# Chunk columns by transposing transfers out of SBUF, row factors by VectorE, inverse sums in halves

## The chip, the cores and the metric

The kernel runs on one core of a Trainium2 chip. The metric is the device time of one execution in microseconds, the median of several runs. TensorE is called PE, VectorE DVE, ScalarE ACT, GpSimd POOL and SyncE SP; SP computes nothing here and issues nearly all transfers (DMAs).

## The reference

With x of 2048 rows by 512 columns (bf16), `xn = layernorm(x)` and `out = x + A(xn) * silu(B(xn))`.

A is sliding-window attention with 32 heads of 16 and a window of eight keys at distances 0, 2, ..., 14:

```python
qkv = xn @ wqkv
logits = einsum("bhsd,bhswd->bhsw", q, k[window]) * 16**-0.5      # -1e9 before row 0
o = einsum("bhsw,bhswd->bhsd", softmax(logits), v[window])
A = o @ wo
```

B is an MLP whose hidden columns are shifted along the rows in four groups (by +1, -1, +2 and -2):

```python
h = gelu(layernorm(xn) @ w1)          # 512 x 512
x1 = xn + shifted(h) @ w2             # 512 x 512
B = x1 + gelu(layernorm(x1) @ w3) @ w4   # 512 x 1376, 1376 x 512
```

## The kernel before, in words

Rows are split by parity, so that a distance of 2 becomes 1 within a half: `xn[0]` holds the 1024 even rows, `xn[1]` the odd ones. Each half has two chunks of 512 rows, four tiles of 128. Chunks 0 and 1 are the even rows, 2 and 3 the odd ones.

The first stage works chunk by chunk. `Norm` takes statistics on DVE (`stats`), the reciprocal root on POOL for chunks 1 to 3 (`root`), and scales on DVE (`apply`). The projections need xn with columns on the partitions, `xnT`; `turn` makes it, two tiles at a time, with eight PE transposes into PSUM and one DVE copy. From xnT come q (`q_all`), k (`k_all`, kept by four ACT instructions with head masks, `kM`), and v (`v_pair`, kept in one of two staging tiles `vst` and written to DRAM as `v_d`). Since B normalises xn a second time, each row gets a further factor: `rows2` computes it on POOL, `rows2_spread` transposes the 128 x 4 factors on PE, copies them with DVE, writes them to DRAM (`r2_d`) and reads them back onto all partitions. `rows2_here` instead multiplies the factors into an identity on DVE and spreads them with a matmul of ones. `scaled` multiplies xnT by them, and `w1` uses the result.

`w2(c)` adds the shifted product to xn in place and takes the statistics of the sum. `columns(c)` scales these rows, writes them to DRAM (`x1n_dram`) and reads them back with one transposing transfer as `x1nT`, which `w3` uses. After `w3(3)` comes the attention stage.

The attention stage is a loop over n of 18 units of 114 queries, nine per half. In iteration n run `scores(n)`, ACT's exponentials, DVE's `band`, `values` of an earlier unit, and pieces of w4 and of the output projection (`g_fin`) between them. The sums of the softmax are gathered for batches of four units (the last batch has two). At the end of a batch (n = 5, 9, 13, 16) `inverse` takes the reciprocal, `write_rec` sends it to DRAM, `read_rec` brings it back spread over the partitions into `rr_t`, and `apply` multiplies it into `oT`; the output projection of the rows follows. The last batch of two units goes through PE (`expand`) after the loop, behind `apply(3)`.

The tile framework keeps each engine's instructions in the order in which they are written, and inserts waits between engines where data depends. SP's queue is also in that order, so a transfer that waits holds up all SP transfers behind it. PSUM has eight banks: three pairs go round (`pair`) in the first stages and two single ones (`single`).

Of the kernel before, what the change touches and what calls it, by code (L numbers as in the profile page):

```python
# [8 lines left out]
AF = mybir.ActivationFunctionType  # L9
# [11 lines left out]
def kernel(  # L21
# [19 lines left out]
    def pin(ins):  # L41

        return tc.keep_in_program_order(ins)
# [52 lines left out]
    def single():  # L96
        cnt["s"] += 1
        return PS[:, 6 + (cnt["s"] - 1) % 2, :]
# [54 lines left out]
    m57 = const.tile([P, QB], BF16, name="m57")  # L153
    e_sb = const.tile([P, 8, 8, 16], BF16, name="e_sb")
    zero = const.tile([P, D], BF16, name="zero")

    def head_masks():
        pin(DVE.tensor_reduce(
# [39 lines left out]
    r2_d = dram.tile([NCH, CH], BF16, name="r2_d")  # L198
    x1n_dram = dram.tile([S, D], BF16, name="x1n_dram")
    vst = [b4([P, 2, 2, D], f"vst{i}") for i in range(2)]  # L200


# [4 lines left out]
    def small_t(name, shape, dt=F32):  # L207
        return small.tile(shape, dt, name=name, tag=name)
# [33 lines left out]
    def x_of(c):  # L242
        p, k = c // 2, c % 2
        return xn[p][:, k * TPC : (k + 1) * TPC, :]
# [3 lines left out]
    def rows2(c, ln):  # L248

        r2 = small_t("r2", [P, TPC])  # L250
        r2b = small_t("r2b", [P, TPC], BF16)
        eng = DVE if c == 0 else POOL
        pin(eng.tensor_tensor(out=r2, in0=ln.rstd, in1=ln.rstd, op=ALU.mult))
        pin(eng.tensor_tensor(out=r2, in0=r2, in1=ln.mv[:, :, 1], op=ALU.mult))
        if c == 0:
            pin(ACT.activation(r2, r2, AF.Sqrt, bias=eps_t[:]))
            with nc.allow_low_precision("bf16 row factors"):
                pin(DVE.reciprocal(out=r2b, in_=r2))
        else:
            rsqrt_eps(r2, r2)  # L260
            pin(POOL.tensor_copy(out=r2b, in_=r2))
        r2s[c] = r2b

    def rows2_spread(c):
        pt = single().bitcast(BF16)[0:TPC, 0:P]
        pin(PE.transpose(pt, r2s[c], ident[:]))
        t = small_t("r2t", [TPC, P], BF16)
        pin(DVE.tensor_copy(out=t, in_=pt))
        pin(SP.dma_start(out=r2_d[c].rearrange("(j q) -> j q", q=P), in_=t))
        xn2Ts[c] = b4([P, ND, CH], "xn2T")  # L270
        pin(SP.dma_start(out=xn2Ts[c][:, ND - 1, :], in_=r2_d[c : c + 1, :].to_broadcast([P, CH])))

    def rows2_here(c):

        xn2Ts[c] = t = b4([P, ND, CH], "xn2T")
        d = t[:, 0, :].rearrange("p (j q) -> p j q", q=P)
        pin(DVE.tensor_tensor(
            out=d, in0=ident.unsqueeze(1).to_broadcast([P, TPC, P]), in1=r2s[c].unsqueeze(2).to_broadcast([P, TPC, P]),
            op=ALU.mult,
        ))  # L280
        pt = single()
        pin(PE.matmul(pt, lhsT=ones_bf[:], rhs=t[:, 0, :], start=True, stop=True))
        if c == 0:
            pin(ACT.activation(t[:, ND - 1, :], pt, AF.Copy))
        else:
            pin(DVE.tensor_copy(out=t[:, ND - 1, :], in_=pt))

    def scaled(c):
        p, k = c // 2, c % 2
# [17 lines left out]
    def turn_one(c, t):  # L307
        p, k = c // 2, c % 2
        i = k * TPC + t
        pt = single().bitcast(BF16)[:, 0 : ND * P].rearrange("p (a q) -> p a q", a=ND)  # L310
        for dt in range(ND):
            pin(PE.transpose(pt[:, dt, :], xn[p][:, i, dt * P : (dt + 1) * P], ident[:]))
        pin(ACT.activation(xnT[p][:, :, i * P : (i + 1) * P], pt, AF.Copy))

    def q_half(pts, lo, hi, nts=range(ND)):
        for nt in nts:
# [28 lines left out]
    def k_pad(p):  # L345
        pin(POOL.memset(kM[p][:, :, 0:8, :], 0.0))
        pin(POOL.memset(kM[p][:, :, M + 8 : MK, :], 0.0))
# [35 lines left out]
        else:  # L383
            later.append(put)

    def v_pair(p, t):
        pt = pair()
        for i in range(2):
            v_mm(p, t + i, pt[:, i, :])
        v_keep(p, t, 2, pt[:, 0, :])  # L390

    def v_pad(p):
        rows = v_d[p].rearrange("r e d -> (r e) d")
# [49 lines left out]
    def columns(c):  # L443
        ln = ln2[c]
        ln.apply(0, TPC)
        pin(SP.dma_start(
            out=x1n_dram[c * CH : (c + 1) * CH, :].rearrange("(i q) d -> q i d", q=P), in_=ln.dst
        ))
        x1nT = b4([P, ND, CH], "x1nT")
        pin(SP.dma_start_transpose(out=x1nT, in_=x1n_dram[c * CH : (c + 1) * CH, :]))  # L450
        x1nTs[c] = x1nT

    h3a, h3b = {}, {}
# [39 lines left out]
    pin(POOL.memset(zero, 0.0))  # L493
    k_pad(0)
    k_pad(1)
    pin(ACT.activation(
# [26 lines left out]
    head_masks()  # L523
    load_x(3, 0, 2)
    load_x(3, 2, 2)
    q_half(pq, 2 * P, CH, (0, 1))
    rows2_here(0)
    q_half(pq, 2 * P, CH, (2, 3))
    for a in range(2):
# [4 lines left out]
    l1.stats(2, 4)  # L534
    l1.root()
    l1.apply(0, 4)
    rows2(1, l1)
    pin(SP.dma_start(out=w2_sb, in_=B_w2.rearrange("(g q) n -> q g n", q=P)))
    k_all(0, (0,))
    v_pair(0, 2)  # L540
    k_all(0, (1,))
    v_pad(0)
    w1(0, 0)
    rows2_spread(1)
    pin(SP.dma_start(out=w3_sb, in_=B_w3.rearrange("(dt q) f -> q dt f", q=P)))
    turn(1, 0)
    turn(1, 1)
    w1(0, 1)
    l2 = Norm(x_of(2), x_of(2), TPC, "l1")
    l2.stats(0, 4)  # L550
    l2.root()
    l2.apply(0, 4)
    rows2(2, l2)
    l3 = Norm(x_of(3), x_of(3), TPC, "l1")
    l3.stats(0, 4)
    l3.root()
    scaled(1)
    q_all(1)
    k_all(1)
    v_pair(0, 4)  # L560
    l3.apply(0, 4)
    rows2(3, l3)
    v_pair(0, 6)
    rows2_spread(2)
    w1(1, 0)
    turn(2, 0)
    turn(2, 1)
    w1(1, 1)
    scaled(2)
    q_all(2)  # L570
    turn(3, 0)
    turn(3, 1)
    k_all(2)
    pin(SP.dma_start(
        out=w4_sb[:, 0 : NF - 1, :],
        in_=B_w4[0 : (NF - 1) * P, :].rearrange("(ft q) n -> q ft n", q=P),
    ))
    pin(SP.dma_start(out=w4_sb[0:FL, NF - 1, :], in_=B_w4[(NF - 1) * P : F, :]))
    rows2_here(3)
    scaled(3)  # L580
    w1(2, 0)
    w1(2, 1)
    w1(3, 0)
    w1(3, 1)
    w2(0)
    columns(0)
    v_pad(1)
    q_all(3)
# [96 lines left out]
    def read_rec(b):  # L685
        pin(SP.dma_start(
            out=rr_t.rearrange("p j a q -> p (j a q)"),
            in_=ap_of(rec_ds[b][:], [[16 * NQ, 16], [0, 8], [1, 16 * NQ]]),
        ))

    def apply(b):
        lo, hi = batches[b]
        n = lo
        while n < hi:
            p, u = n // UP, n % UP
            m = min(hi, (p + 1) * UP) - n
            x = oT[p][:, :, u * NQ : (u + m) * NQ].rearrange("p a (j q) -> p a j q", q=NQ)
            rr = rr_t[:, n - lo : n - lo + m].rearrange("p j a q -> p a j q")
            pin(DVE.tensor_tensor(out=x, in0=x, in1=rr, op=ALU.mult))
            n += m  # L700
# [177 lines left out]
    for n in range(NU):  # L878
        now["n"] = n
        q = W4 * (n + 1) // NU - given  # L880
        given += q
        extra = small_g.get(n, [])
        if n == 0:
            w4_take(HEAD)

        if n - 1 in ends:
            read_rec(ends[n - 1])
        if n == 15:
            values(13)
# [7 lines left out]
        if n in xo_at:  # L897
            load_xo(*xo_at[n])
        if n == 4:
            load_wo()  # L900
        if n - 1 not in ends:
            flush_stores(n - 2)
        flush(vstores)
# [88 lines left out]
```

## Time and profile before

| | before |
|---|---|
| median of 3 runs | 197.72 us (197.51 to 197.74) |
| profiled execution | 197.26 us |
| its span, first to last instruction | 195.5 us |
| granted PE clock | 0.996 |
| busy PE, DVE, ACT, POOL | 185.5, 117.8, 133.3, 19.1 us |
| DMA | 28.12 MB in 33576 packets |

The stages of the span: the first projections, w1 and w2 up to 70.8 us, w3 (with the last w2) from 70.8 to 112.4, attention with w4 from there to about 185, and the last output groups to the end. In rows of the profile an instruction is named by its line and engine, then output <- inputs; a count follows with x, and brackets hold the idle time of the engine before it and what ended that.

### The profile page before, as it was taken

The numbers are of one execution on the slowest core, as the hardware profiler recorded it, in microseconds if no ns is written. First come the engines' busy times: TensorE is split into PE (matmuls) and PEld (weight loads), VectorE is DVE, ScalarE is ACT, GpSimd is POOL, SyncE is SP. The second block draws the span as 40 slices with busy tenths as digits, with TensorE's granted clock in tenths as the row PEclk, the third lists the DMA queues.
The fourth block names the chain that finished last, engine by engine and source line by source line (L and its number), as shares of the span: only waits on it lengthen the run. The fifth ranks groups of instructions, "written<-read, shape, count | busy, mean of one in ns | idle before, by whom it ended". The sixth has DMA issues, their size and how long they took to land.

```text
span 195.5 us, 5255 instructions
## 1 busy us (share of the span) xinstructions
PE 185.5 (95%) x2253; PEld 91.8 (47%) x2283; DVE 117.8 (60%) x229; ACT 133.3 (68%) x151; POOL 19.1 (10%) x57
## 2 busy tenths in 40 slices
PE   7899999999999999999999999999999999999990
PEld 2474544554444444444444444445444544554540
DVE  5785767236076697494200035556487888798894
ACT  7399769649817615435656588877887876887871
POOL 3006066100002022006000000000000000000000
PEclk9999999999999999999999999999999999999998
DMA  4997480654000433752480051457565556582523
GB/s 131 339 368 239 132 282 15 218 158 157 0 0 3 136 83 109 215 107 65 110 260 0 0 162 60 157 166 232 153 216 161 137 155 215 127 247 51 171 91 126
DMA packets 33576, 28.12 MB, mean 144 GB/s; under 512 B 10760, under 2 KB 32528, under 8 KB 33552
## 3 DMA queue, kind: packets, MB, share of 16 engines
q1 hardware_dynamic: 33408, 27.71, 47.2%
q8 instruction: 18, 0.29, 0.6%
q10 hardware_dynamic: 144, 0.07, 0.1%
q14 instruction: 6, 0.05, 0.1%
HBM read 17.01 MB, written 8.67 MB: 131 GB/s over the span
## 4 chain that ended last, share of the span: by engine, by line
PE 85%; DMA 5%; DVE 4%; issue 2%; SPq 1%; ACT 1%
PE PS L469 19%; PE PS L328 19%; PE PS L764 19%; PE PS L427 5%; PE PS L811 4%; PE PS L795 4%; PE PS L652 3%; DMA wqk_sb<-in_A_wqkv_dram 3%; PE PS L626 3%; PE PS L362 3%; DMA x1nT<-x1n_dram 2%; PE PS L318 2%; PE PS L662 2%; PE PS L302 2%; DVE sg L825 2%
## 5 line engine op out<-in xcount | busy, mean ns | idle before, releaser
L469 PE MATMUL PS<-x1nT,w_sb 128*128 128x512 bf16 (+1 forms) x173 | 38.2, 379 | 0.4 <-DMA x1nT<-x1n_dram 0.3
L633 ACT ACTIVATE prob<-PS 128x1824 bf16<-128x1824 f32 x18 | 30.4, 1688 | 4.4 <-PE PS L626 3.6
L764 PE MATMUL PS<-w_sb,h3a 128*128 128x512 bf16 x112 | 29.2, 379 | 1.9 <-issue 1.7
L475 ACT ACTIVATE h3a<-PS 128x1024 bf16<-128x1024 f32 x16 | 16.4, 1024 | 21.0 <-PE PS L469 19.1
L777 DVE TENSOR_TENSOR xn<-PS,xn 128x512 bf16<-128x512 f32 x15 | 10.3, 686 | 32.0 <-PE PS L764 31.8
L469 PEld LDWEIGHTS <-w_sb 128*128 128x128 bf16 (+1 forms) x176 | 17.5, 100 | 20.9 <-issue 0.7
L328 PE MATMUL PS<-xnT,wqk_sb 128*128 128x512 bf16 x109 | 25.0, 379 | 0.2
L354 ACT ACTIVATE kM<-PS,em 128x1024 bf16<-128x1024 f32 x16 | 20.8, 1404 | 3.2 <-PE PS L328 3.2
L638 DVE TENSOR_TENSOR prob<-prob,maskb 128x1824 bf16<-128x1824 bf16 x18 | 19.8, 1102 | 1.8 <-ACT prob L633 1.8
L764 PEld LDWEIGHTS <-h3a 128*128 128x128 bf16 x128 | 11.3, 97 | 13.4 <-issue 1.2
L328 PEld LDWEIGHTS <-wqk_sb 128*128 128x128 bf16 x112 | 10.9, 98 | 12.8
L435 DVE TENSOR_TENSOR xn<-PS,xn 128x1024 bf16<-128x1024 f32 x8 | 9.6, 1213 | 11.3 <-PE PS L427 11.3
L811 PE MATMUL PS<-wo_sb,oT 128*128 128x512 bf16 (+1 forms) x68 | 15.5, 366 | 0.0
L328 PE MATMUL PS<-xn2T,w_sb 128*128 128x512 bf16 x62 | 14.6, 379 | 0.1
L427 PE MATMUL PS<-w_sb,hT 128*128 128x512 bf16 x63 | 14.4, 379 | 0.1
L821 ACT ACTIVATE sg<-PS 128x512 bf16<-128x512 f32 (+1 forms) x17 | 9.6, 572 | 6.1 <-PE PS L811 6.1
L764 PE MATMUL PS<-w_sb,h3b 128*128 128x512 bf16 (+1 forms) x44 | 12.8, 380 | 0.8 <-issue 0.8
L339 ACT ACTIVATE qT<-PS 128x1024 bf16<-128x1024 f32 x8 | 8.1, 1024 | 7.6 <-PE PS L328 7.6
L373 ACT ACTIVATE vst<-PS 128x512 bf16<-128x512 f32 (+1 forms) x12 | 8.8, 743 | 3.5 <-ACT sig L784 2.3
L221 DVE BATCH_NORM_STATS2 l1s<-xn 128x6 f32<-128x512 bf16 x16 | 10.1, 680 | 1.6 <-DMA xn<-in_A_x_dram 1.6
L400 ACT ACTIVATE hT<-PS 128x1024 bf16<-128x1024 f32 x8 | 8.1, 1031 | 3.8 <-PE PS L328 3.8
L221 DVE BATCH_NORM_STATS2 l3s<-xn 128x6 f32<-128x512 bf16 x16 | 10.2, 682 | 0.2
(105 smaller groups left out, 229.2 us busy)
## 6 DMA issues: line engine op xcount, KB each, us to landing
ring<-v_d SPq DMA_DIRECT2D x18, 256.0 KB, 3.3
v_d<-vst SPq DMA_DIRECT2D x16, 256.0 KB, 2.7
x1n_dram<-xn SPq DMA_DIRECT2D x4, 512.0 KB
xo<-in_A_x_dram SPq DMA_DIRECT2D x8, 256.0 KB, 4.1
ring<-rec_d SPq DMA_DIRECT2D x4, 456.0 KB, 4.7
out_dram<-xo SPq DMA_DIRECT2D x7, 256.0 KB
xn<-in_A_x_dram SPq DMA_DIRECT2D x6, 256.0 KB, 7.9
w_sb<-in_B_w_dram SPq DMA_DIRECT2D x1, 1376.0 KB
```

The costliest lines, as they stand in the source:

```text
L221: pin(DVE.bn_stats(out=self.st[:, j, :], in_=self.src[:, j, :]))
L328: pin(PE.matmul(pt[:, b, :], lhsT=w[:, dt, nt * P : (nt + 1) * P], rhs=rhs[:, dt, :], start=(dt == 0), stop=(dt == ND - 1),))
L354: pin(ACT.activation(kM[p][:, 2 * a : 2 * a + 2, 8 + k * CH : 8 + (k + 1) * CH, e], pt, AF.Copy, scale=em[:, e : e + 1]))
L427: pin(PE.matmul(pt[:, j, :], lhsT=w2_src(p, g, m0), rhs=w2_sb[:, g, :], start=(g == 0), stop=(g == ND - 1),))
L435: pin(DVE.tensor_tensor(out=xs, in0=pts[h], in1=xs, op=ALU.add))
L469: pin(PE.matmul(pt[:fs, ft % 2, :], lhsT=w3_sb[:, dt, ft * P : ft * P + fs], rhs=x1nT[:, dt, :], start=(dt == 0), stop=(dt == ND - 1),))
L475: pin(ACT.activation(t[:, o : o + 2, :], pt, AF.Gelu_apprx_tanh))
L633: pin(ACT.activation(pr, S_ps[:, :, 0 : ND * NQ], AF.Exp, scale=SCALE))
L638: pin(DVE.tensor_tensor(out=f, in0=f, in1=maskb[:], op=ALU.min))
L764: pin(PE.matmul(pt, lhsT=h3_of(c, ft)[:fs, jj * P : (jj + 1) * P], rhs=w4_sb[:fs, ft, :], start=(ft == 0), stop=(ft == NF - 1 and silu < 2),))
L777: pin(DVE.tensor_tensor(out=x_i, in0=pt, in1=x_i, op=ALU.add))
L811: pin(PE.matmul(pt[:, 0:W], lhsT=oT[p][:, dt, i * P : (i + 1) * P], rhs=wo["sb"][:, dt, c], start=(dt == 0), stop=(dt == ND - 1),))
```

## The change

- xnT of chunks 1 to 3 is made by `turn_dma`: one transposing transfer per tile, SBUF to SBUF, issued by SP. `turn` on PE remains for chunk 0 alone.
- `columns` transposes each tile straight from SBUF, four transfers of 128 x 512 instead of one write to DRAM and one transposing read of 512 x 512. `x1n_dram` is gone.
- Row factors of chunks 1 to 3 are put into a zeroed tile `r2p`, transposed in blocks of 32 by DVE and written to DRAM (`rows2_write`), and read back spread (`rows2_read`). Chunk 3 no longer uses `rows2_here`.
- The order of the first stage is new: v of tiles 4 to 7 comes before q and k of chunk 1; the writes of v are collected in `vputs` and issued after the transposes; w2_sb is loaded earlier and w3_sb later; `w2(0)` stands before `w1(3, 1)`.
- In the attention loop `read_rec` and `apply` work on two units at a time, one iteration apart, for batches 0 to 2. Batch 2's second half is applied at the end of n = 16. The writes of v, the loads of x for the output and the stores stand at the end of the iteration.

```diff
+    r2p = const.tile([P, NCH, 32], BF16, name="r2p")
...
-    def rows2_spread(c):
-        pt = single().bitcast(BF16)[0:TPC, 0:P]
-        pin(PE.transpose(pt, r2s[c], ident[:]))
-        t = small_t("r2t", [TPC, P], BF16)
-        pin(DVE.tensor_copy(out=t, in_=pt))
-        pin(SP.dma_start(out=r2_d[c].rearrange("(j q) -> j q", q=P), in_=t))
+    def rows2_write(c):
+        t = small_t("r2t", [P, 32], BF16)
+        pin(DVE.transpose(out=t, in_=r2s[c]))
+        pin(SP.dma_start(out=ap_of(r2_d[c], [[32, P // 32], [P, 32], [1, 32]]), in_=t))
+
+    def rows2_read(c):
         xn2Ts[c] = b4([P, ND, CH], "xn2T")
...
+    def turn_dma(c, lo=0, hi=TPC):
+        p, k = c // 2, c % 2
+        for t in range(lo, hi):
+            i = k * TPC + t
+            pin(SP.dma_start_transpose(out=xnT[p][:, :, i * P : (i + 1) * P], in_=xn[p][:, i, :]))
...
     def columns(c):
         ln.apply(0, TPC)
-        pin(SP.dma_start(
-            out=x1n_dram[c * CH : (c + 1) * CH, :].rearrange("(i q) d -> q i d", q=P), in_=ln.dst
-        ))
         x1nT = b4([P, ND, CH], "x1nT")
-        pin(SP.dma_start_transpose(out=x1nT, in_=x1n_dram[c * CH : (c + 1) * CH, :]))
+        for t in range(TPC):
+            pin(SP.dma_start_transpose(out=x1nT[:, :, t * P : (t + 1) * P], in_=ln.dst[:, t, :]))
...
     l1.apply(0, 4)
+    turn_dma(1)
     rows2(1, l1)
-    pin(SP.dma_start(out=w2_sb, in_=B_w2.rearrange("(g q) n -> q g n", q=P)))
+    vputs = []
     k_all(0, (0,))
-    v_pair(0, 2)
+    v_pair(0, 2, vputs)
     k_all(0, (1,))
-    v_pad(0)
-    w1(0, 0)
-    rows2_spread(1)
-    pin(SP.dma_start(out=w3_sb, in_=B_w3.rearrange("(dt q) f -> q dt f", q=P)))
-    turn(1, 0)
-    turn(1, 1)
-    w1(0, 1)
     l2 = Norm(x_of(2), x_of(2), TPC, "l1")
     l2.stats(0, 4)
+    rows2_write(1)
+    vputs.pop(0)()
     l2.root()
     l2.apply(0, 4)
+    rows2_read(1)
     rows2(2, l2)
+    w1(0, 0)
+    w1(0, 1)
+    v_pair(0, 4, vputs)
+    v_pair(0, 6, vputs)
+    turn_dma(2)
     l3 = Norm(x_of(3), x_of(3), TPC, "l1")
     l3.stats(0, 4)
     l3.root()
+    rows2_write(2)
     scaled(1)
     q_all(1)
     k_all(1)
-    v_pair(0, 4)
     l3.apply(0, 4)
     rows2(3, l3)
-    v_pair(0, 6)
-    rows2_spread(2)
+    turn_dma(3, 0, 2)
+    rows2_read(2)
+    rows2_write(3)
+    turn_dma(3, 2, 4)
+    rows2_read(3)
+    while vputs:
+        vputs.pop(0)()
+    v_pad(0)
+    pin(SP.dma_start(out=w3_sb, in_=B_w3.rearrange("(dt q) f -> q dt f", q=P)))
     w1(1, 0)
-    turn(2, 0)
-    turn(2, 1)
     w1(1, 1)
     scaled(2)
     q_all(2)
-    turn(3, 0)
-    turn(3, 1)
     k_all(2)
+    scaled(3)
...
-    rows2_here(3)
-    scaled(3)
     w1(2, 0)
     w1(2, 1)
     w1(3, 0)
+    w2(0)
     w1(3, 1)
-    w2(0)
     columns(0)
...
-        if n - 1 in ends:
-            read_rec(ends[n - 1])
+        if n == NU - 1:
+            read_rec(3)
+        for j in range(2):
+            if n - 1 - j in ends and n < NU - 1:
+                read_rec(ends[n - 1 - j], 2 * j, 2)
...
         if n == 15:
-            apply(ends[n - 2])
+            apply(2, 0, 2)
...
-        if n < 15 and n - 2 in ends:
-            apply(ends[n - 2])
+        for j in range(2):
+            if n < 15 and n - 2 - j in ends:
+                apply(ends[n - 2 - j], 2 * j, 2)
+        if n == 16:
+            apply(2, 2, 2)
         if n >= 15:
             flush(late)
             flush(gates)
         while extra:
             extra.pop(0).all()
+
+        flush(vstores)
+        if n in xo_at:
+            load_xo(*xo_at[n])
+        flush_stores(n - 2)
```

The last three steps stood before `inverse` and `write_rec` in the same iteration, and stores were left out in the iteration behind the end of a batch.

More of the change, by code (lines that the diff above doesn't have):

```diff
@@ L197 @@
     v_d = [dram.tile([MK, 2, D], BF16, name=f"v_d{p}") for p in range(2)]
-    r2_d = dram.tile([NCH, CH], BF16, name="r2_d")
-    x1n_dram = dram.tile([S, D], BF16, name="x1n_dram")
+    r2_d = dram.tile([NCH, 32 * P], BF16, name="r2_d")
     vst = [b4([P, 2, 2, D], f"vst{i}") for i in range(2)]
@@ L250, in rows2 @@
         r2 = small_t("r2", [P, TPC])
-        r2b = small_t("r2b", [P, TPC], BF16)
         eng = DVE if c == 0 else POOL
@@ L256, in rows2 @@
             pin(ACT.activation(r2, r2, AF.Sqrt, bias=eps_t[:]))
+            r2b = small_t("r2b", [P, TPC], BF16)
             with nc.allow_low_precision("bf16 row factors"):
@@ L260, in rows2 @@
             rsqrt_eps(r2, r2)
-            pin(POOL.tensor_copy(out=r2b, in_=r2))
+            r2b = r2p[:, c, :]
+            pin(POOL.tensor_copy(out=r2b[:, 0:TPC], in_=r2))
         r2s[c] = r2b
-    def rows2_spread(c):
-        pt = single().bitcast(BF16)[0:TPC, 0:P]
-        pin(PE.transpose(pt, r2s[c], ident[:]))
-        t = small_t("r2t", [TPC, P], BF16)
-        pin(DVE.tensor_copy(out=t, in_=pt))
-        pin(SP.dma_start(out=r2_d[c].rearrange("(j q) -> j q", q=P), in_=t))
+    def rows2_write(c):
[3 more added lines that the diff above has]
+    def rows2_read(c):
         xn2Ts[c] = b4([P, ND, CH], "xn2T")
-        pin(SP.dma_start(out=xn2Ts[c][:, ND - 1, :], in_=r2_d[c : c + 1, :].to_broadcast([P, CH])))
+        pin(SP.dma_start(out=xn2Ts[c][:, ND - 1, :], in_=r2_d[c : c + 1, 0:CH].to_broadcast([P, CH])))
     def rows2_here(c):
@@ L282, in rows2_here @@
         pin(PE.matmul(pt, lhsT=ones_bf[:], rhs=t[:, 0, :], start=True, stop=True))
[L283 to L286, printed above, removed]
+        pin(ACT.activation(t[:, ND - 1, :], pt, AF.Copy))
     def scaled(c):
@@ L384, in v_keep, with v_pair @@
             later.append(put)
-    def v_pair(p, t):
+    def v_pair(p, t, later=None):
         pt = pair()
@@ L389, in v_pair @@
             v_mm(p, t + i, pt[:, i, :])
-        v_keep(p, t, 2, pt[:, 0, :])
+        v_keep(p, t, 2, pt[:, 0, :], later)
     def v_pad(p):
@@ L493 @@
     pin(POOL.memset(zero, 0.0))
+    pin(POOL.memset(r2p, 0.0))
     k_pad(0)
@@ L525 @@
     load_x(3, 2, 2)
+    pin(SP.dma_start(out=w2_sb, in_=B_w2.rearrange("(g q) n -> q g n", q=P)))
     q_half(pq, 2 * P, CH, (0, 1))
@@ L683, in write_rec, with read_rec, apply @@
             pin(SP.dma_start(out=ap_of(rec_d[:], [[32 * NQ, 8], [NQ, 16], [1, NQ]], 16 * NQ * k), in_=recs[b]))
-    def read_rec(b):
+    def read_rec(b, j=0, w=4):
         pin(SP.dma_start(
-            out=rr_t.rearrange("p j a q -> p (j a q)"),
-            in_=ap_of(rec_ds[b][:], [[16 * NQ, 16], [0, 8], [1, 16 * NQ]]),
-        ))
-    def apply(b):
-        lo, hi = batches[b]
-        n = lo
+            out=rr_t[:, j : j + w].rearrange("p j a q -> p (j a q)"),
+            in_=ap_of(rec_ds[b][:], [[16 * NQ, 16], [0, 8], [1, 4 * w * NQ]], 4 * j * NQ),
+        ))
+    def apply(b, j=0, w=4):
+        lo = batches[b][0]
+        n, hi = lo + j, lo + j + w
         while n < hi:
@@ L896 @@
             load_va(n + 1)
-        if n in xo_at:
-            load_xo(*xo_at[n])
         if n == 4:
             load_wo()
-        if n - 1 not in ends:
-            flush_stores(n - 2)
-        flush(vstores)
         if n != 16:
```

## The prediction

> **What bounds the kernel now.** I read the page's first two parts, then the chain in order of time, then stretches of the timeline for SP, DVE and ACT, and windows of a microsecond where the chain left PE.
>
> ```profile
> span 195.5 us, 5255 instructions
> PE 185.5 (95%) x2253; PEld 91.8 (47%) x2283; DVE 117.8 (60%) x229; ACT 133.3 (68%) x151; POOL 19.1 (10%) x57
> ...
> PE   7899999999999999999999999999999999999990
> ...
> PE 85%; DMA 5%; DVE 4%; issue 2%; SPq 1%; ACT 1%
> ```
>
> PE is busy in every slice but the first and the last, and 85% of the chain is PE. So a PE instruction taken out between those two slices shortens the run, as long as its operands stay early. The clock leaves nothing more: it is granted in full. The windows by stage (PE, PEld, DVE, ACT, POOL busy, clock, DMA share, GB/s) say the same of the attention stage:
>
> ```profile
> 112.40:164.00 51.60, 49.58 (x1187) 25.57 (x1199) 34.19 (x48) 41.93 (x50) 0.00 (x0) 1.00 0.54 161
> 164.00:185.00 21.00, 20.16 (x490) 10.68 (x494) 17.65 (x28) 17.05 (x24) 0.00 (x0) 1.00 0.58 165
> ```
>
> Spreading SP's work there can win little: PE has 2.9 us of gaps in 72.6, most of them short waits that the profile calls issue. I count nothing for it, and up to 0.3 either way for the range.
>
> **What leaves PE.** The chain in order of time (start, length, what):
>
> ```profile
> 15.07 1.73 PE PS L362 x8
> 16.80 3.45 PE PS L328 x16
> 20.25 0.15 PE PS L266
> 20.40 1.00 PE PS L302 x16
> ...
> 33.48 0.15 PE PS L266
> ...
> 35.46 0.89 PE PS L302 x16
> ...
> 41.54 0.89 PE PS L302 x16
> 42.43 3.45 PE PS L328 x16
> 45.88 0.22 PE PS L282
> ...
> 66.16 4.51 DMA x1nT<-x1n_dram
> ```
>
> L302 are the turns of chunks 1, 2 and 3, L266 the two transposes of row factors, L282 the matmul that spreads chunk 3's factors. All become transfers or DVE work: 0.15 + 1.00 + 0.15 + 0.89 + 0.89 + 0.22 = 3.30 us off the chain. DVE also loses six copies out of PSUM, but it is not the bound there.
>
> The last row is w3(0) waiting for its columns. Windows of one microsecond there:
>
> ```profile
> 66.00:67.00 1.00, 0.92 (x5) 0.37 (x4) 0.97 (x2) 0.87 (x1) 0.00 (x0) 1.00 0.00 0
> 67.00:68.00 1.00, 1.00 (x6) 0.41 (x6) 1.00 (x5) 0.00 (x0) 0.00 (x0) 1.00 0.30 71
> ...
> 70.00:71.00 1.00, 0.73 (x4) 0.17 (x3) 1.00 (x4) 0.00 (x0) 0.23 (x1) 1.00 0.07 14
> ```
>
> PE is idle 0.27 us from 70 to 71. In the new kernel columns(0) transposes straight out of SBUF, without the write to DRAM (63.17 to 66.16 below), and w2(0) stands one w1 half (1.73 us) earlier. The columns are then some 5 us ahead of w3(0), and I take 0.3 off. Together -3.6.
>
> **What the transfers cost.** They cost PE nothing if they land in time. The SP rows and what feeds them:
>
> ```profile
> 63.17 0.39 SPq L446 DMA_DIRECT2D x1n_dram<-xn  x1
> ...
> 66.16 2.20 SPq L450 DMA_TRANSPOSE x1nT<-x1n_dram  x1
> ```
> ```profile
> L450 SPq DMA_TRANSPOSE x1nT<-x1n_dram x4: 1308/1980/2202, 66.2 to 94.9; - x4
> ```
> ```profile
> 17.37 1.38 DVE L237 TENSOR_SCALAR xn<-xn,l1m,l1r 128x512 bf16<-128x512 bf16 x4 [1.48 <-POOL l1r L205]
> ...
> 18.66 1.36 SPq L377 DMA_DIRECT2D v_d<-vst  x2
> ```
>
> The trace has transposing transfers of 512x512 from DRAM, none of 128x512 from SBUF. Call x the time that one of the new ones holds SP. Below it is bounded by a plain issue, 0.39; above by the longest whole one, 2.20, since a quarter of the work should not cost more than all of it. I take the plain issue plus a quarter of the rest of the median 1.98, 0.39 + 0.40 = 0.8, being nearest in bytes; the shortest, 1.31, stays in the range. The whole one landed 4.51 us after its issue, and its data ran from about 67.7 to 70.1; a quarter of that data would save 1.8, so a small one lands about 2.7 after its issue. Between these points, landing = 1.65 + 1.3x.
>
> The place that is tight is chunk 1. DVE finishes its first tile at about 17.8, and SP is free by then. PE now goes from w1(0,0) (ends 20.25) through w1(0,1), 1.73, to v_pair(0,4) at 21.98 and v_pair(0,6) at 23.70, whose last tile is read at 24.6. The fourth transfer is issued at 17.8 + 3x and lands at 19.45 + 4.3x. PE waits 4.3x - 5.1: nothing at x = 0.8 (landing 22.9), nothing until x = 1.2, 0.5 at 1.31, 2.3 at 1.7, 4.3 at 2.20.
>
> Loads in flight would come first, but they are done when the transfers begin:
>
> ```profile
> 18.60:19.00 0.40, 0.40 (x3) 0.17 (x2) 0.16 (x1) 0.40 (x2) 0.40 (x1) 1.00 0.00 0
> ```
>
> A page of the Trainium skill speaks against this change. "VectorE: DVE Perf Modes", section "The three transpose paths", gives 1309 ns for a 128x128 block by DMA and 390 by TensorE, and its rules prefer TensorE where a PSUM destination will do. Read per block, its estimate for a tile of four is 5.2 us, and the sum would be a loss of some 15 us instead of a gain. The trace does not bear that out: sixteen blocks landed in 4.51 us.
>
> Behind these transfers on SP wait rows2_write(1), the two v_d writes of v_pair(0,2) (1.36) and rows2_read(1). The writes free vst[1] for v_pair(0,6): at x = 0.8 they are issued by about 23.2 and ACT waits perhaps half a microsecond at 25.4, where PE has two PSUM pairs in hand. rows2_read(1) is wanted by scaled(1) before w1(1,0) at about 32.3, and is issued near 23.7. For chunks 2 and 3 the factors are read at about 30 and 33 and wanted at 42.7 and 46.1; without this slack of ten, x = 2.20 would cost 1.4 more at w1(3,0). w3 and w4 start loading near 36, wanted after 67. DVE's transposes of factors and POOL's memset of r2p are each some tenths, on engines with idle time there, and cost nothing.
>
> **What becomes late next.** PSUM is emptied by ACT, and k is its slow part:
>
> ```profile
> 44.20 5.17 ACT L354 ACTIVATE kM<-PS,em 128x1024 bf16<-128x1024 f32 x4 [1.60 <-PE PS L328]
> ```
>
> k_all(2) started on PE at 42.43 (its 16 matmuls end at 45.88), so its second pair is free 6.94 after the start. With turn and rows2_here gone, two pieces of 3.45 lie between that start and the next use of the pair, 6.90. That happens at q_all(2) and at w1(3,0): I add 0.1 each, 0.2.
>
> **The end of the run.** Here I expect a loss. apply(2) was one step at n = 15; now its second half comes at the end of n = 16, after flush(finals). read_rec(3), first on SP at n = 17, overwrites the half of rr_t which that step reads, so it has to wait for it. The timeline:
>
> ```profile
> 178.77 0.56 SPq L686 DMA_DIRECT2D ring<-rec_d  x1
> ...
> 179.02 0.43 DVE L831 TENSOR_TENSOR xo<-sg,xo 128x512 bf16<-128x512 bf16 x1
> ...
> 180.27 1.03 PE L811 MATMUL PS<-wo_sb,oT 128*128 128x512 bf16 x4
> 180.28 1.11 DVE L638 TENSOR_TENSOR prob<-prob,maskb 128x1824 bf16<-128x1824 bf16 x1 [0.83 <-ACT prob L633]
> ...
> 182.55 0.87 DVE L674 RECIPROCAL rec<-PS 128x114 bf16<-128x114 f32 x1 [0.56 <-PE PS L662]
> ...
> 183.56 1.11 DVE L699 TENSOR_TENSOR oT<-oT,ring 128x1824 bf16<-128x1824 bf16 x1
> ...
> 184.59 0.42 DVE L825 TENSOR_TENSOR sg<-sg,xn 128x512 bf16<-128x512 bf16 x1
> ...
> 185.66 0.84 DVE L719 TENSOR_TENSOR oT<-oT,rk 128x456 bf16<-128x456 bf16 x2 [0.20 <-ACT rk L713]
> ...
> 186.60 0.42 DVE L825 TENSOR_TENSOR sg<-sg,xn 128x512 bf16<-128x512 bf16 x1
> ...
> 192.46 0.29 DVE L831 TENSOR_TENSOR xo<-sg,xo 128x256 bf16<-128x256 bf16 x1
> ```
> ```profile
> DMA to landing us min/median/max: 4.7/4.7/4.8
> ```
>
> The last row is read_rec's: issued at 178.77 it lands near 183.5, and apply(3) starts at 183.56. On the times of before, the finals end at 179.45; the moved half, 912 columns at a rate of 1.11 for 1824 with some fixed part, takes about 0.63 and ends at 180.1, just in DVE's gap before 180.28 and just ahead of the PE group at 180.27 that reads it. read_rec(3) is then issued near 180.2 instead of 178.77, lands near 184.95, and apply(3) starts 1.4 late. From there DVE runs almost without a gap to 192.75, so the end moves: 1.4 less the two small gaps (0.20 before 185.66, 0.1 before 186.60) is 1.1. At least 0, if the half ran before 178.8; at most 1.4. The halves of batches 0 and 1 are applied an iteration ahead of the output groups that read them and cost nothing; if that cover of several microseconds were gone, each would stop PE by its 0.6.
>
> **Sum.** -3.3 - 0.3 + 0.2 + 1.1 = -2.3. The profiled execution took 197.26 (span 195.5 and 1.76 around it), which gives 195.0. The runs' median is 197.72, 0.46 above it, so I predict 195.4.
>
> **Rivals.** *The end does not move*: the waiting read finds its slot free, as it would were the half done earlier. The fixed order on DVE speaks against it. Then -3.4: 194.3.
>
> *Transfers a little long*, x from 1.2 to 1.7: PE waits at v_pair(0,4) and (0,6) for 0 to 2.3, giving 195.4 to 197.7. For it speaks that even the shortest DMA_TRANSPOSE held SP 1.31; if that is a fixed price, the stall is 0.5 and the time 195.9.
>
> *Transfers long: slower.* If a small one holds SP as long as a whole one, the fixed part being nearly all of it, chunk 1's last tile lands at 28.9 and PE loses 4.3, and the factors of chunk 3 are 1.4 late on the crowded queue: 195.4 + 5.7 = 201.1. It turns into a loss at x = 1.7. For it: four issues replace one, and three of four whole ones took about 2 us. Against it: the spread from 1.31 to 2.20 at one size looks like a queue filling, which a quarter would not do. Its far end is a price per 128-column block: at the 1.31 of the shortest row for each of four, x is 5.2, PE waits 4.3 x 5.2 - 5.1 = 17, and the time passes 212. The 4.51 for sixteen blocks leaves this 0.02 of the chance. (That is the reading of the skill's page above, "VectorE: DVE Perf Modes".)
>
> *ACT becomes the bound*: k takes ACT 5.17 where PE needs 3.45; if the pieces after k did not cover the 1.7 difference for chunks 1 and 2, up to 3.2 comes back beyond my 0.2: 195.4 to 198.6. Against it speaks the count of 6.90 against 6.94.
>
> **Chances and range.** Forecast 0.47; end unmoved 0.11; a little long 0.14; long 0.20; ACT 0.08. A measurement here tells about 0.2%, 0.4 us, from no change. Faster by more: 0.47 + 0.11 + 0.12 of the third + 0.03 of the last = 0.73. Within: 0.02 + 0.02 = 0.04. Slower: 0.20 + 0.03 = 0.23. The forecast's own range is 194.8 to 196.1 (the end's bounds of 0 to 1.4 in part, 0.3 in attention). For 8 in 10 I go from 194.0, below the second case, to 199.0, into the fourth; the upper part of the fourth, above 0.1, is left out.
>
> **What would show it.** PE should have no transposes after the first chunk, and the w3 stage should start near 67.1 instead of 70.8. DMA_TRANSPOSE should appear 28 times with a median near 0.8 on SP; over 1.2, PE's wait for xnT at v_pair shows it. read_rec(3) should be issued right behind the half apply, with apply(3) waiting for it and DVE busy from there to the end. I am wrong if PE waits for xnT or xn2T by a microsecond or more, or if apply(3) follows the last reciprocal at once.

## The result and the profile after: 195.67 us against 197.73 us

The changed kernel takes 195.67 us (median of four runs, 195.29 to 199.22; one run stood apart at 199.22 and is not in the ratio), the kernel before 197.73 us. The ratio is 0.9884, 95% interval 0.9852 to 0.9916: about 2.3 us less (the two medians are 2.06 apart). The forecast was 195.4 us, range 194.0 to 199.0. The profiled execution took 195.73 us with a span of 194.0 at a granted clock of 0.997, so it is compared with the 195.5 of the span before. The page of the changed kernel, its head and the head of its chain:

```profile
span 194.0 us, 5210 instructions
PE 182.0 (94%) x2203; PEld 89.0 (46%) x2232; DVE 112.5 (58%) x225; ACT 133.1 (69%) x151; POOL 19.5 (10%) x58
...
PE 68%; DVE 10%; ACT 8%; DMA 7%; issue 3%; SPq 1%; POOL 1%
```

PE lost 50 instructions and 3.5 us of busy time, but the span lost only 1.5. To see where the rest went, four places of PE's timeline were read in each kernel: the first q matmul, the first matmul of w3, the first attention score, and the expand after the last inverse. All lengths in us of the span:

| kernel | first q at | q to w3 | w3 to score | score to expand | expand to end |
|---|---|---|---|---|---|
| before | 8.94 | 61.86 | 42.83 | 70.77 | 11.10 |
| after | 9.57 | 58.73 | 42.83 | 71.71 | 11.16 |

The last column goes by the span, which the page gives to 0.1. So the first stage gained 3.13, the attention stage lost 0.94, the end lost 0.06, and the first q came 0.63 later, behind a load of wqk_sb. SP issues the same loads in the same order ahead of it in both kernels. Over all profiles of this case the first q comes at 8.77 to 8.94 with the old first stages and at 8.50 to 10.86 with the new ones; why it varies is open. PE's timeline of the changed kernel, with the idle time ahead of a row in brackets:

```profile
25.31 1.04 PE L367 MATMUL PS<-wv_sb,xnT 128*128 128x512 bf16 x4 [0.34 <-DMA xnT<-xn]
...
47.36 0.81 PE L333 MATMUL PS<-xn2T,w_sb 128*128 128x512 bf16 x3 [0.29 <-ACT kM L359]
...
68.30 0.59 PE L472 MATMUL PS<-x1nT,w_sb 128*128 128x512 bf16 x2
...
171.90 0.35 PE L661 MATMUL PS<-prob,ring 128*32 128x57 bf16 x21
173.09 0.27 PE L661 MATMUL PS<-prob,ring 128*32 128x57 bf16 x11 [0.84 <-issue]
```

There are two new short waits in the first stage (the last xnT tile of chunk 1, and w1(3,0) behind k_all(2); both are shorter than they look, see below), no wait ahead of w3, and one wait of 0.84 in the middle of the 32 small matmuls of values(15), at n = 16, for which the profile names nothing. The transposing transfers on SP (count, shortest, median and longest in ns):

```profile
L318 SPq DMA_TRANSPOSE xnT<-xn x12: 1189/1216/1307, 18.4 to 37.5; - x12
```
```profile
L453 SPq DMA_TRANSPOSE x1nT<-xn x16: 1191/1218/2382, 58.4 to 91.5; - x16
```

28 of them, as forecast, but 1.22 us each by the median, not 0.8, and a single one up to 2.38, above the bound of 2.20. The end, DVE and SP:

```profile
177.79 0.62 DVE L708 TENSOR_TENSOR oT<-oT,ring 128x912 bf16<-128x912 bf16 x1
...
182.88 1.11 DVE L708 TENSOR_TENSOR oT<-oT,ring 128x1824 bf16<-128x1824 bf16 x1 [1.02 <-DMA ring<-rec_d]
...
190.93 0.29 DVE L840 TENSOR_TENSOR xo<-sg,xo 128x256 bf16<-128x256 bf16 x1
```
```profile
178.44 0.57 SPq L695 DMA_DIRECT2D ring<-rec_d  x1
```

read_rec(3) is issued right behind the half apply (178.41), and apply(3) waits 1.02 for it, as forecast. Yet the distance from the expand to the end is the same.

### The profile page after: what moved, and what is told of

Same layout as the page of the kernel before. It is cut to its first block, busy times and chain, and to the rows that moved or that the text cites. A ratio compares the mean times of both kernels' runs of the same rounds, so it can differ in the third digit from the quotient of the medians.

```text
span 194.0 us, 5210 instructions
## 1 busy us (share of the span) xinstructions
PE 182.0 (94%) x2203; PEld 89.0 (46%) x2232; DVE 112.5 (58%) x225; ACT 133.1 (69%) x151; POOL 19.5 (10%) x58
## 4 chain that ended last, share of the span: by engine, by line
PE 68%; DVE 10%; ACT 8%; DMA 7%; issue 3%; SPq 1%; POOL 1%
PE PS L472 20%; PE PS L773 17%; PE PS L333 10%; ACT kM L359 8%; PE PS L432 5%; PE PS L804 4%; DMA wqk_sb<-in_A_wqkv_dram 3%; PE PS L820 3%; PE PS L661 3%; PE PS L635 3%; DVE l1s L221 2%; DMA ring<-rec_d 2%; DVE xo L840 2%; DVE sg L834 2%; PE PS L671 2%
## 5 line engine op out<-in xcount | busy, mean ns | idle before, releaser
L290 DVE TENSOR_TENSOR xn2T<-xnT,xn2T 128x2048 bf16<-128x2048 bf16 x4 | 4.9, 1217 | 10.7 <-DMA xn2T<-r_d 7.4
```

## Experiments

Ratios are to the kernel before, run alongside on the same chip, with 95% intervals. All kernels compute the whole reference. The lengths that the verdicts use, from the profiles in the same way as above (the stall is a wait of PE inside a group of values matmuls, in e6 of the sums behind them, with nothing named for it except in e4; e5's transfers are those of e10):

| kernel | q to w3 | PE's wait for xnT | score to expand | stall | expand to end |
|---|---|---|---|---|---|
| before | 61.86 | none | 70.77 | 0.11 | 11.10 |
| after | 58.73 | 0.34 | 71.71 | 0.84 | 11.16 |
| e1 first stages | 58.92 | 0.53 | 70.73 | none | 10.96 |
| e2 attention | 62.20 | none | 70.59 | none | 11.11 |
| e3 whole change | 59.39 | 0.81 | 71.82 | 0.81 | 11.53 |
| e4 batch 2 whole | 58.95 | 0.55 | 72.18 | 0.85, for DVE | 11.17 |
| e6 chunk 1 by PE | 61.56 | 2.06, for DVE's copy | 71.08 | 0.35 | 10.84 |
| e7 shifted | 58.97 | 0.38 | 70.52 | none | 11.13 |
| e9 before, late apply | 62.24 | none | 71.27 | 0.59 | 12.15 |
| e10 wide and shifted | 58.43 | none | 71.29 | 0.45 | 10.96 |
| e11 small shift | 58.88 | 0.47 | 71.51 | 0.55 | 11.09 |
| e12 before, shifted | 62.95 | none | 70.59 | none | 11.09 |
| e13 x1nT by DRAM | 59.94 | 1.23 | 72.21 | 1.38 | 11.21 |

w3 to the first score is 42.82 to 42.84 in every one of them.

Two things about waits help to read these numbers. Matmuls overlap: four take 1.04 us and two 0.59 in PE's timeline above, so one is 0.38 long and starts 0.22 after the one before, and a wait costs the stage about 0.16 more than the idle time of its row. And some matmul records are missing. The group that w1(3,0) belongs to, in the changed kernel and in e7:

```profile
L333 PE MATMUL PS<-xn2T,w_sb 128*128 128x512 bf16 x62 | 14.4, 379 | 0.3 <-ACT kM L359 0.3
```
```profile
L333 PE MATMUL PS<-xn2T,w_sb 128*128 128x512 bf16 x64 | 14.6, 379 | 0.1
```

Both have 64 weight loads. Of the 0.29 ahead of w1(3,0), 0.22 is a matmul whose record is missing just there; in e7, with all records, the wait is 0.06, and one of 0.05 stands ahead of q_all(2). The wait for xnT is too long by the same 0.22 in the rows of the changed kernel, e1, e4 and e11, so its true range over the kernels with one tile per transfer is 0.1 to 1.2.

**The change in two.** e1 has the new first stages and the old read_rec, apply and order of the attention loop; e2 the reverse; e3 is the whole change again.

```
e1:  the new kernel up to w4;   read_rec(b), apply(b) whole, SP's order in the loop as before
e2:  the old kernel up to w4;   read_rec/apply in halves, SP's order as changed
```

> The first stages as changed (transposing transfers, row factors by VectorE, new order), the attention loop as before (whole reads and applies, SP's work in the old places). Theory A: the first stages win 3.0 us on PE (3.3 of instructions and 0.3 of idle less 0.6 of new waits at the v of chunk 1 and at w1(3,0)), and the new attention loop gives about 0.9 of it back. Then this kernel takes about 194.7, faster than the changed kernel by 0.9, w3 starts near 68, and the stretch from the start of w3 to the end takes about 124.7 as before. Rival B: the attention loop is neutral and the 0.9 in the profile was chance; the first stages win only 2.1. Then 195.6, level with the changed kernel.

> The first stages as before, the attention loop as changed. Theory A: slower than before by about 0.9 (198.6), because the read of the third batch waits for the half apply at n = 16 and PE has a new wait in that iteration. Rival B: level with before, 197.7 within 0.3. The prediction's own step (the end moves 1.1 later): 198.8.

> The changed kernel once more, unaltered, for a second profile. Theory A: 195.6; PE's wait of 0.8 inside the values of n = 16 is there again, and the first q starts at about 9.0 instead of 9.57, since no edit touches the loads ahead of it. If the wait is gone and the total is lower by as much, it was chance. Rival: the late first q is the change's own, and recurs.

Measured: e1 195.95 us, ratio 0.9912 [0.988, 0.9944]; e2 197.17, 0.9969 [0.9943, 0.9994]; e3 195.95, 0.9899 [0.9865, 0.9933]. The first stages carry nearly all of it, and the two parts add up within the intervals. By the times the rivals hold: e1 is level with e3, not 0.9 below it, and e2 is no slower than before. So the loss in the attention stage, which e1's profile lacks (70.73 against 71.82 in e3), is not seen in e1's median; the first q of that profile comes 1.9 later than e3's (10.86 against 8.93). In e3 both waits stand again (0.81 each), and the late first q does not. e2 shows the end by itself. Its timeline (DVE, then SP), to be held against the prediction's rows of before:

```profile
179.36 0.63 DVE L699 TENSOR_TENSOR oT<-oT,ring 128x912 bf16<-128x912 bf16 x1
...
184.53 1.11 DVE L699 TENSOR_TENSOR oT<-oT,ring 128x1824 bf16<-128x1824 bf16 x1 [1.11 <-DMA ring<-rec_d]
...
192.59 0.29 DVE L831 TENSOR_TENSOR xo<-sg,xo 128x256 bf16<-128x256 bf16 x1
```
```profile
180.01 0.56 SPq L686 DMA_DIRECT2D ring<-rec_d  x1
```

apply(3) starts 0.97 later than before (184.53 against 183.56), at the same place of the expand (184.39 against 184.40), but the last row is only 0.13 later (192.59 against 192.46). So the delay is real and the end hardly follows it.

**Is the late end's price zero, and why?** e4 takes the delay out of the changed kernel; e9 puts a larger one into the kernel before.

```diff
# e4, on the changed kernel
-            apply(2, 0, 2)          # n == 15, and apply(2, 2, 2) at n == 16
+            apply(2)                # n == 15, after one read_rec(2) at n == 14
# e9, on the kernel before
     rec = inverse()
+    for i in range(2):              # 2.2 us of DVE work, on the mask, which stays as it is
+        DVE.tensor_tensor(out=maskb, in0=maskb, in1=maskb, op=min)
     apply(3)
```

> The changed kernel with batch 2 read whole at n = 14 and applied whole at n = 15 as before, so that the read of batch 3 at n = 17 no longer waits for a half apply at n = 16; batches 0 and 1 stay in halves. The prediction's step: the end comes 1.1 earlier, 194.5. Theory A: DVE's late start at the end is caught up, since ACT and PE set the pace of the last output groups; the read lands 1 us earlier and the time moves by 0.3 at most, 195.3 to 195.7, unless PE's wait at n = 16 comes from the same place, in which case 0.9 less.

> The kernel before, with two more VectorE steps of 128x1824 (1.1 us each, on a tile that is not used any more) ahead of apply(3), so that VectorE reaches it 2.2 us later. The prediction's step, VectorE is the bound from there to the end: the stretch from the expand matmuls to the end grows by 1.9 to 2.2, from 11.1 to 13.1, and the time to 199.8. Theory A, ACT and PE pace the last output groups and VectorE has about 1 us of slack: it grows by 1.0 to 1.3, to 12.2, and the time to 198.9.

Measured: e4 196.02 us, 0.9908 [0.9874, 0.9942], no better than e3; e9 199.09, 1.0062 [1.0034, 1.0089]. In e4 apply(3) follows the last reciprocal at once, and expand to end is 11.17, as in the changed kernel. So against the changed kernel's profile there was no loss to be won back, against e3's 0.4. e4 also pays for the whole read elsewhere: on DVE's timeline apply(2) waits for it ahead of the mask step, and PE 0.85 for that step.

```profile
170.38 1.18 DVE L708 TENSOR_TENSOR oT<-oT,ring 128x456 bf16<-128x456 bf16 x2 [1.16 <-DMA ring<-rec_d]
171.48 1.10 DVE L647 TENSOR_TENSOR prob<-prob,maskb 128x1824 bf16<-128x1824 bf16 x1
```

e9's timeline, DVE and then PE:

```profile
186.20 1.10 DVE L699 TENSOR_TENSOR oT<-oT,ring 128x1824 bf16<-128x1824 bf16 x1
...
194.24 0.29 DVE L831 TENSOR_TENSOR xo<-sg,xo 128x256 bf16<-128x256 bf16 x1
```
```profile
187.36 5.36 PE L811 MATMUL PS<-wo_sb,oT 128*128 128x512 bf16 x28 [0.78 <-DVE oT L699]
```

e3, where the read came later than in the changed kernel's profile (DVE, then PE):

```profile
183.36 1.11 DVE L708 TENSOR_TENSOR oT<-oT,ring 128x1824 bf16<-128x1824 bf16 x1 [1.36 <-DMA ring<-rec_d]
```
```profile
183.37 6.52 PE L820 MATMUL PS<-wo_sb,oT 128*128 128x512 bf16 x32
```

Measured from each kernel's own expand, apply(3) starts 0.84 before it in the kernel before (183.56, 184.40), 0.04 after it in the changed kernel, 0.39 after it in e3 (183.36, 182.97), and 1.05 after it in e9 (186.20, 185.15). The first shift, of 0.88, moves the end by 0.06; the second, of 1.23, by 0.43; the third, of 1.89, by 1.05. PE waits for oT in the last two alone (in e3 its output groups take 6.52, in the changed kernel 6.22). So there is a slack of about 0.8 to 0.85, and what goes beyond it moves the end in full. It lies in small gaps of DVE, which keeps step with PE and ACT when it is early; ACT's timeline of the kernel before:

```profile
186.78 0.60 ACT L821 ACTIVATE sg<-PS 128x512 bf16<-128x512 f32 x1 [0.21 <-PE PS L811]
187.65 0.60 ACT L821 ACTIVATE sg<-PS 128x512 bf16<-128x512 f32 x1 [0.27 <-PE PS L811]
188.45 0.60 ACT L821 ACTIVATE sg<-PS 128x512 bf16<-128x512 f32 x1 [0.20 <-PE PS L811]
189.31 0.60 ACT L821 ACTIVATE sg<-PS 128x512 bf16<-128x512 f32 x1 [0.27 <-PE PS L811]
```

PE's output groups come 0.80 to 0.87 apart. DVE's two steps for a group, once it is behind, come 0.79 apart (L825 at 189.42, 190.21 and 191.01 in e9). From the step behind apply(3) to the start of its last row DVE takes 7.87 in the kernel before (184.59 to 192.46) and 7.02 in the changed kernel (183.91 to 190.93) and in e9 (187.22 to 194.24): 0.85 of its time there was waiting. A late DVE catches up; an early one looks busy because it keeps step.

**The price of a transposing transfer.** e5 lays xnT and x1nT out tile by tile, so that one transfer turns two tiles of xnT, or four of x1nT. e6 turns chunk 1 on PE again.

```diff
# e5, on the changed kernel (the matmuls read the same columns from the new layout)
-    xnT = [b8([P, ND, M], f"xnT{p}") for p in range(2)]
+    xnT = [b8([P, M // P, ND, P], f"xnT{p}") for p in range(2)]
-        for t in range(lo, hi):
+        for t in range(lo, hi, 2):      # one transfer for two tiles, 128 x 1024
# e6, on the changed kernel
-    turn_dma(1)
     w1(0, 0)
+    turn(1, 0)
+    turn(1, 1)
     w1(0, 1)
```

> The changed kernel with xnT and x1nT laid out tile by tile, so that one transposing transfer turns two tiles of xnT (256 KB) and one turns all four of x1nT (512 KB): 6 and 4 transfers in place of 12 and 16. The 128x512 ones held SP 1.19 to 1.31 us each and landed 2.4 after issue. Theory A, a price per transfer: two tiles hold SP 1.2 to 1.5, four 1.3 to 2.2 as those out of DRAM did; chunk 1 is turned 2 us sooner, PE's wait of 0.3 to 0.8 at its v is gone, and the time falls by about that, to 195.4. Rival, a price per byte: 2.4 and 4.8 each, PE waits as long as before and for the first two tiles too, 196 or more.

> The changed kernel, but chunk 1 turned by PE and VectorE's copies again between the two halves of w1(0), as before. If the transfers of chunk 1 were hidden (the prediction), this costs the 16 transposes, 0.9 to 1.0 us: 196.9. With the wait of 0.3 to 0.8 at the v of chunk 1 that the profiles show, it costs 0.2 to 0.6: 196.2 to 196.5. If SP's queue held up more than that behind the four transfers, it gains.

Measured: e5 194.81 us, 0.983 [0.979, 0.987]; e6 197.84, 0.9987 [0.9951, 1.0023]. PE nowhere waits for xnT in e5, nor in e10 below, which has the same transfers. Their SP rows in e10:

```profile
L318 SPq DMA_TRANSPOSE xnT<-xn x6: 1232/1264/1349, 18.2 to 32.0; - x6
```
```profile
L460 SPq DMA_TRANSPOSE x1nT<-xn x4: 1675/1902/2002, 58.5 to 87.7; - x4
```

By the medians two tiles hold SP for 1.26 us, four for 1.90, one for 1.22: nearly a fixed price per transfer. Halving the number took PE's wait for xnT away. e5's time fell by more than the wait, but its interval touches e3's at its end (0.987 and 0.9865), and the two were measured at different times, on different chips. e6 lies outside all that was expected of it. It is no clean test of the 0.89 that chunk 1's turn costs, as its waits show:

```profile
PE PS L367 <- DVE xnT L302: 2.1, 1, 2.1
```

The copies out of PSUM stand behind DVE's statistics of the next chunk, which the new order has put ahead of them, so PE waits 2.1 us. It shows only that the new order and PE's turn do not go together.

**The unnamed wait in values(15).** e7 and e11 put small matmuls on PE ahead of the first projection, where PE waits for weights anyway; each is two places of PE's program (a load and a matmul), so that everything later moves by 64 or 16 places. e12 does the same to the kernel before.

```diff
# e7, e10 and e12: 32 of them; e11: 8; into a PSUM bank that is not yet in use
+    for i in range(32):
+        r = 32 * (i % 4)
+        PE.matmul(PS[r:r+32, 7, 0:QB], lhsT=ones_bf[:, 0:32], rhs=ones_bf[:, 0:QB], tile_position=(0, r))
     q_half(pq, 0, 2 * P, (0, 1))
```

> The changed kernel with 32 more small matmuls (32 columns, 57 moving) on a free PSUM bank right ahead of the first q, where PE waits for wqk anyway; they move every later PE instruction by 64 places. Theory F: PE's wait of 0.8 inside the values of n = 16 (after 21 of 32 matmuls, nothing that the profile names) is PE running out of fetched instructions. Then it moves 32 matmuls ahead, to the 22nd matmul of the scores of n = 16, or vanishes, being behind 1.4 us of long matmuls; the time falls by up to 0.8. Rival: the wait is one for data or a bank of that matmul; it stays at the 22nd matmul of the values, and the time does not change (0.0 to 0.3 more).

> The changed kernel with 8 small matmuls ahead of the first projection: TensorE's later instructions stand 16 places later in its program. Theory that the unnamed wait belongs to a place of TensorE's program (a boundary at which further instructions have to come in): the wait of about 0.8 us stands 8 matmuls earlier, after 13 of the 32 of values(15) at n = 16 instead of after 21, the place at which the kernel before has it; the time as the changed kernel's, ratio 0.988 to 0.990. Rival, that it belongs to the data (prob, the ring or the PSUM bank): it stays after 21 of 32. Second rival, that it is random: it is absent, and the ratio about 0.984.

> The kernel before with the same 32 small matmuls ahead of the first projection, which stand while TensorE waits for the first weights. If they cost and gain nothing by themselves, the time is that of the kernel before but for its small wait at 158.5 us of the span, 0.1 to 0.6 us, which goes elsewhere: ratio 0.997 to 1.000. If the matmuls themselves help (a warmer clock, say), the ratio is near 0.994, what they gave the changed kernel, and the theory of the place in the program loses its best evidence.

Measured: e7 194.75 us, 0.9828 [0.9793, 0.9862]; e11 195.6, 0.9899 [0.9868, 0.9931]; e12 199.14, 1.0051 [1.0024, 1.0078]. (The expectations count from about 1.3 us ahead of the first score.) e7 has no such wait, and its score to expand, 70.52, is the shortest of all; its interval lies below that of e3, which was measured at another time. e11's timeline:

```profile
171.88 0.29 PE L667 MATMUL PS<-prob,ring 128*32 128x57 bf16 x13
172.72 0.33 PE L667 MATMUL PS<-prob,ring 128*32 128x57 bf16 x19 [0.55 <-issue]
```

The wait has moved from after 21 to after 13 of the 32 matmuls: 8 earlier for 8 added, as the theory of a place in PE's program said. e9, which has the kernel before's PE program, has its wait in an earlier group, values(10), after 13 of 32, at 159.38 and 0.59 long; the kernel before lost 0.11 at that very place. So the place is fixed by the program and the length varies. In e13 and e5, which have twelve and eighteen transposing transfers fewer than e3 (and so other waits in PE's program), it stands after 24 and after 25.

e12 contradicts the second half of its expectation: the shift took the wait away (70.59), and yet the kernel became slower. So the added matmuls do not help by themselves. What is longer shows in the profile of its one profiled run, PE and then DVE:

```profile
46.76 0.38 PE L282 MATMUL PS<-xn2T,ones_bf 128*128 128x512 bf16 x1 [0.98 <-DVE xn2T L277]
```
```profile
43.69 1.23 DVE L291 TENSOR_TENSOR xn2T<-xnT,xn2T 128x2048 bf16<-128x2048 bf16 x1 [6.55 <-DMA xn2T<-r_d]
```

The factors of chunk 2 come back from DRAM 4.3 us after the issue of their read at 39.4, where it was 3.1 in the kernel before (39.3 to 42.37). DVE then reaches chunk 3's factors late and PE waits 0.98 for them; e9 shows 0.34 of the same. Whether the added matmuls cause the late landing, or only that run had it, is open.

**Both waits out, and the other columns.** e10 is e5 and e7 together; e13 makes x1nT by way of DRAM again.

```diff
# e13, on the changed kernel
-        for t in range(TPC):
-            SP.dma_start_transpose(out=x1nT[:, :, t * P : (t + 1) * P], in_=ln.dst[:, t, :])
+        SP.dma_start(out=x1n_dram[c * CH : (c + 1) * CH, :].rearrange("(i q) d -> q i d", q=P), in_=ln.dst)
+        SP.dma_start_transpose(out=x1nT, in_=x1n_dram[c * CH : (c + 1) * CH, :])
```

> The changed kernel with both edits that took a wait of TensorE away: two tiles of a chunk by one transfer (four of x1nT), and 32 small matmuls ahead of the first projection, which shift TensorE's later instructions by 64 places. Theory: the two waits are independent (xnT at chunk 1's value products, 0.3 to 0.8 us; the unnamed one inside values(15), 0.8 us), so both are gone: no wait for xnT on TensorE, values(15) at n = 16 in one run of 32 matmuls or with a wait under 0.1, from the first attention score to the expand 71.8 us (73.1 to 73.4 where the unnamed wait stood), time 194.3 (194.0 to 194.8), ratio to the kernel before about 0.980. Rival: the earlier gains of these two kernels were scatter of the first loads, and the time is that of the changed kernel, 195.7 to 196.0, ratio 0.989 to 0.990.

> The changed kernel with the second kind of columns, x1nT, made as before: x1n written to DRAM and read back by one transposing transfer of a chunk, while xnT keeps its transfers out of SBUF. If that part of the change is worth nothing, since w2 of the chunk before stands between, the time is the changed kernel's, 195.7 to 196.0, ratio 0.988 to 0.990, and TensorE waits for x1nT at w3 only as in the kernel before (0.3 us at chunk 0). If the shorter path carries part of the gain (the 0.3 at w3 of chunk 0 that the forecast booked), the ratio is 0.990 to 0.992.

Measured: e10 194.54 us, 0.9847 [0.9817, 0.9877]; e13 196.04, 0.9902 [0.9866, 0.9938]. e10 has the lowest median of the study, 1.06 below that of e11, which was measured with it, and no wait for xnT; but a wait in the values stands at another place (0.45, at 155.75, in values(10)), presumably because fewer transfers move the program too. Its interval overlaps e5's and e7's, so that the two edits add up is not shown. e13's ratio lies at the border of its two expectations and decides nothing, but its trace has no wait ahead of w3: the shorter path of x1nT is worth nothing once w2(0) stands earlier.

## Why the prediction was right

The time came within 0.3 us, and for the first stage the working holds. That the total came so near was luck: the loss booked at the end did not come, and losses that were not foreseen took its place.

**The removed PE work, -3.30, and w3's wait, -0.3: right.** No transposes are left behind chunk 0, and the wait of 0.27 is gone. With 0.2 added, the forecast for the stage was -3.4, with which w3 would start at 67.4, not at the 67.1 given as a sign. In e10, which has no wait for xnT, q to w3 is 3.43 shorter than before. The agreement is closer than the noise: e2 has the first stages of the kernel before and takes 0.34 longer for them. Of the two causes named for the 0.3, e13 shows that the earlier w2(0) is enough; the shorter path of x1nT is not needed for it.

**x, the time a small transfer holds SP: too low.** I scaled it by bytes, 0.8; it is 1.22, next to the shortest row of before (1.31), which I kept for the range. The reason I gave for that choice, that the spread from 1.31 to 2.20 looked like a queue filling, was wrong for the small ones: the price is mostly fixed. By my own formula 1.22 gives a wait of 0.15 and 1.31 gives 0.5. By the rows PE waited 0.34 to 0.81 in six profiles of the one-tile transfers and 1.23 in e13 (0.22 less in four of them, where a record is missing). The first transfer was issued as forecast (18.44, with the first q 0.63 late, against 17.8). But it held SP longer than the others, and the wait grows with that: 1.31 us and a wait of 0.34 in the changed kernel, 1.74 and 0.81 in e3, 2.16 and 1.23 in e13. Why the first one is long is open. Hence the rival "a little long" is what happened in this place, at its mild end. The Trainium skill's 1309 ns for one block ("VectorE: DVE Perf Modes", "The three transpose paths") is near what a transfer of four blocks costs here; taken per block it is refuted by e10's 1.90 us for sixteen.

**New PSUM waits, +0.2: right in place.** Both came, at q_all(2) and at w1(3,0). Where no record is missing (e7) they are 0.05 and 0.06 of idle time; with the 0.16 that a wait costs beyond it, about 0.2 each where 0.1 was forecast.

**The late end, +1.1: wrong in its last step.** The half apply, the wait of read_rec(3) and apply(3)'s delay came as written (0.97 in e2, forecast 1.4). "From there DVE runs almost without a gap" failed: I counted two gaps, 0.3 in all, where DVE kept step with PE's groups and had about 0.85 in hand. So the end moved 0.13 in e2 and 0.06 in the changed kernel; in e3, where the read landed later, it moved 0.43. The rival "the end does not move" was nearly right about the end, but not for its reason: the read did wait.

**What was not foreseen: +0.9 in values(15).** Score to expand is 70.5 to 70.8 where no or hardly any stall shows, and 71.08 to 72.21 in those with one of 0.35 to 1.38: 0.1 to 0.5 more than the stall itself (e4 apart). In the changed kernel's profile the stage is 0.94 longer, most of it this stall. In that profile it took the place of the loss I had booked at the end. That it costs the medians as much is not shown: e7, without it, is faster than e11, measured at another time, and e1, without it in its profile, is not faster than e3. The spreading of SP's attention work, counted as nothing, is worth 0.2 by e2's 70.59 against 70.77, where a stall of 0.11 is gone; e2's ratio is 0.06% to 0.6% below 1.

In sum, for the profiled executions: +0.63 (first load) - 3.13 + 0.94 + 0.06 = -1.5, where -2.3 was forecast. The medians differ by 2.06, 0.5 more, because the kernel before's profiled run lies 0.46 below its median and the changed kernel's 0.06 above. The prediction added 0.46 to come from profile to median; that offset did not recur, and it made up for most of what the profile had lost.

## What to carry to other kernels

A busy engine at the end of a chain is not yet the one that sets the pace: measure its steps when it is early and when it is late, and look whether the engine ahead of it waits on another. A transposing transfer out of SBUF costs its queue nearly the same for one tile as for two (1.22 and 1.26 us here), so give each several tiles. And when an engine's program gets longer or shorter, a stall at a fixed place of it can appear or vanish in a stage that the edit never touched; shift the program by a few harmless instructions before blaming the edit.

## What the runs showed of the hardware

PE can stop for 0.1 to 1.4 us inside a run of small matmuls, with nothing that it waits for in the profile (0.11 in the kernel before, 1.38 in e13). The stop stands at a fixed place of its program and moves with it, instruction for instruction (e11). The page of the changed kernel has a queue that brings instructions, 0.28 MB in 17 packets, so about 16 KB each:

```profile
q8 instruction: 17, 0.28, 0.6%
```

That PE runs out of program while such a piece is on its way fits the place, the shift and the varying length; that it is this was not shown directly.

The some 2.4 us of "issue" waits ahead of w_sb in the attention loop, which the prediction took for gaps of PE, are records that are missing. In the changed kernel's groups and in e7's, the same matmuls:

```profile
L773 PE MATMUL PS<-w_sb,h3a 128*128 128x512 bf16 x112 | 29.2, 379 | 1.9 <-issue 1.6 <-DMA v_d<-vst 0.2
```
```profile
L779 PE MATMUL PS<-w_sb,h3a 128*128 128x512 bf16 x128 | 32.7, 380 | 0.0
```

Sixteen records more (and four of h3b) and no gap at all, with the stage as long as in e2 and e12, which lack the same records (70.52 against 70.59). So PE had even less idle time there than the prediction said. Both count 128 weight loads, which shows it without another run: more weight loads than matmuls means that records are missing.
